# Attention followed by SwiGLU on one core: buffers laid out from both ends of SBUF, and a new order of the handover

## The chip, the cores and the metric

The kernel runs on one core of one Trainium2 chip. The metric is the device time of one execution in microseconds (us). Engines are named as the profile names them: PE is the matrix engine (PEld its weight loads), DVE the vector engine, ACT the scalar engine, POOL the GpSimd engine, SP the engine whose queue issues the DMAs (SPq). The five run side by side and wait for one another through semaphores only.

## The reference

Attention with rotary embedding over 4 batches of 8 heads (576 tokens, head size 64), and on its output, laid out as 2304 tokens of width 512, a gated feed-forward of width 1536:

```python
q_rot, k_rot = rotate(q), rotate(k)
scores = D ** -0.5 * q_rot @ k_rot.swapaxes(-1, -2)
scores = scores - scores.max(-1, keepdims=True)
attn = np.exp(scores); attn = attn / (attn.sum(-1, keepdims=True) + 1e-09)
x = (attn @ v).transpose(0, 2, 1, 3).reshape(B * S, H * D)     # 2304 x 512
g = x @ w_gate                                                  # 512 x 1536, float64 weights
out = (g * sigmoid(g) * (x @ w_val)) @ w_out                    # 1536 x 512
```

q, k and v are float32; the kernel is handed the three weight matrices as 64-bit numbers.

## The kernel before

Every product is made of three matmuls (or of two, where a stacked operand holds both parts) on operands cut in a high part `h` and a low part `l`: hi x hi, hi x lo, lo x hi. The cut is a copy to a narrower format (ACT, or POOL for x), and a subtraction.

**Attention.** Two heads make a pair; there are 16 pairs of 9 blocks of 128 queries, n = 0 to 143, p = n // 9 and b = n % 9. For each block PE makes the scores (`scores`, L351), DVE their maximum (`peak`, L366, tile nmt), ACT the exponential (`exp`, L384), PE four transposes (`trans`, L427), ACT the high part and DVE the low part of them (L428, L429, tiles ET1 and ET2). The products with v (`pv`, L467) stand in a list of closures, ten to a PSUM bank, and are taken from it a few in each block; ACT copies the result (`pv_evac`, L472, tile Y), and SP stores it to DRAM (`store`, L486 to L492, tensor yd). A small transpose and store of the reciprocal row sums follows each batch (`rstore`, tensor rd). While a pair runs, POOL rotates q and k two pairs ahead (`rope`) and splits the next v (`vsplit`); PE, ACT and DVE cut the next q and k, which eight DMAs rearrange (`qk_stack`, QK<-N). The buffers N, QK, BD and QZ exist twice, one set for even pairs, one for odd.

**Work for the feed-forward that runs beside attention.** The order in which it is taken stands in PLAN. `cl` and `cvs`: the two converted weight matrices of the first f-tile (f = 0, 128 of the 1536 columns) are loaded and converted in pairs 0 to 3 (`wfirst`). One conversion (`bits`, L608 to L616) turns a 64-bit weight tile into two 32-bit ones with six DVE operations, one ACT copy and two POOL operations. `xs` and `xe`: the first half of the tokens (s = 0, three tiles of 384, four chunks of 128 rows each) is loaded from yd and, with the reciprocals R from rd, made ready by four POOL operations per chunk (`xload`, `xprep`, L594 to L600), between pair 4 and the beginning of pair 15.

**The handover.** At n = 144 attention's tail is placed (the last transposes, the last two rounds of `pv`, the last `rstore`), from there on ACT and DVE issue in the order of the text; POOL does so all through. Then attention's pools are closed, the feed-forward's are opened in the memory that they held, and `first_group` runs f-tiles 0 and 1, with PE in the order of the text. It loads and converts the weights of f = 1 and both `w_out` tiles (`wconv`, each with its nine operations in line), loads the whole second half of the tokens (s = 1) into the accumulator tiles (`stage`, L550, acc<-yd, 768 KB for each of six DMAs) and makes it ready in steps called `scale` and `cut` on POOL, DVE and ACT. `gv` is one tile of the first layer: twelve matmuls g, twelve matmuls v (L660), then on ACT the activation sg (L665), on DVE h = v x sg (L666), on ACT the high and on DVE the low part (L669, L670). g and v have two PSUM buffers each, so a g two tiles on waits for sg, and a v for h. `down` is a tile of the second layer (L684).

**Groups 1 to 5** repeat `gv` and `down` for two f-tiles each, from about 390 us to the end.

Of the kernel before, what the change touches and what calls it, by code (L numbers as in the profile page):

```python
# [34 lines left out]
    order=["qk", "scores", "trans", "pv", "exp", "evac", "rstore", "rope", "tails", "conv", "x", "vsplit"],  # L35
# [67 lines left out]
class Attn:  # L103
    def __init__(self, tc, ctx, q, k, v, tab, yd, rd):
# [3 lines left out]
        pool = lambda name, bufs, **kw: ctx.enter_context(tc.tile_pool(name=name, bufs=bufs, **kw))  # L108
        self.tab_src = tab
        self.x_p = pool("a_x", 2)  # L110
        self.rot_p = pool("a_rot", 2)
        self.t_p = pool("a_t", 1)
        one = pool("a_one", 1)
        self.tab = one.tile([128, 2, 9, D], FP32, name="tabs")
        self.VR = one.tile([128, 10, D], FP32, name="VR")
        self.N, self.QK, self.BD, self.VS, self.QZ = [], [], [], [], []

        def pairbufs(i):
# [4 lines left out]
        pairbufs(0)  # L123
        self.VS.append(one.tile([128, 10, 128], F32R, name="VS0"))
# [3 lines left out]
        one = pool("a_two", 1)  # L128
        pairbufs(1)
# [16 lines left out]
        self.sc_p = pool("a_sc", 2, space=PS)  # L146
        self.tr_p = pool("a_tr", PLAN["trb"], space=PS)
        self.pv_p = pool("a_pv", 4 - PLAN["trb"], space=PS)
# [329 lines left out]
    def store(self, p, half, Y):  # L478
        d = self.nc.sync.dma_start
# [25 lines left out]
class Moe:  # L505
    def __init__(self, tc, keep, yd, rd, wg, wv, wo, out):
# [4 lines left out]
        self.xh = {0: xs.tile([128, NCH, SG], F32R, name="xh0")}  # L511
        self.xl = {0: xs.tile([128, NCH, SG], F32R, name="xl0")}
        self.ld_p = pool("m_ld", 2)
        self.r_p = pool("m_r", 1)
        self.R = None
        self.staged = {}
        self.wpool = xs
        self.Wb = [self.wbuf(0), None]
        self.W, self.Hh, self.Hl = {}, {}, {}

    def wbuf(self, k):
        return [[self.wpool.tile([128, 512], F32R, name=f"w{i}{x}{k}") for x in "hl"] for i in range(2)]

    def open(self, ctx):
        tc = self.tc
        pool = lambda name, bufs, **kw: ctx.enter_context(tc.tile_pool(name=name, bufs=bufs, reuse_waits="tile", **kw))
        self.raw_p = pool("m_raw", 3)
        self.ax_p = pool("m_ax", 2)
        self.wpool = pool("m_w1", 1)
        self.Wb[1] = self.wbuf(1)  # L530
        self.s_p = pool("m_s", 2)
        accs = [pool("m_acc0", 1)]
        self.h_p = [pool("m_h0", 1)]
        xs = pool("m_x1", 1)
        self.xh[1] = xs.tile([128, NCH, SG], F32R, name="xh1")
        self.xl[1] = xs.tile([128, NCH, SG], F32R, name="xl1")
        self.h_p.append(pool("m_h1", 1))
        accs += [pool(f"m_acc{t}", 1) for t in (1, 2)]
        self.wo_p = pool("m_wo", 3)
        PS = bass.MemoryType.PSUM  # L540
        self.g_ps = pool("m_g", 2, space=PS)
        self.v_ps = pool("m_v", 2, space=PS)
        self.d_ps = pool("m_d", 4, space=PS)
        self.acc = [a.tile([128, 6, DM], FP32, name="acc") for a in accs]

    def stage(self, t):
        X = self.acc[t].rearrange("p t d -> p (t d)").rearrange("p (g q) -> p g q", q=384)
        o = SG + t * 384
        for h in range(2):
            self.nc.sync.dma_start(out=X[64 * h:64 * h + 64],  # L550
                                   in_=self.yd[h, :, :, o:o + 384].rearrange("g d q -> d g q"))
        self.staged[t] = X

    def xload(self, s, c, t):
        nc = self.nc
        o = s * SG + t * 384
        if s == 0:
            X = self.ld_p.tile([128, 2, 384], FP32, name="Xab")
            for h in range(2):
                P = slice(64 * h, 64 * h + 64)  # L560
                nc.sync.dma_start(out=X[P], in_=self.yd[h, 2 * c:2 * c + 2, :, o:o + 384].rearrange("a d q -> d a q"))
        else:
            X = self.staged[t][:, 2 * c:2 * c + 2]
        if self.R is None or self.R[0] != (s, t):
            R = self.r_p.tile([128, NCH * 384], FP32, name="R").rearrange("p (c n) -> p c n", c=NCH)
            b0, b1 = 2 * s, 2 * s + 1
            parts = {0: [(b0, 0, 384, 0)], 1: [(b0, 384, 128, 0), (b1, 0, 256, 128)],
                     2: [(b1, 256, 256, 0), (b0, -1, 64, 256), (b1, -1, 64, 320)]}[t]
            for b, col, n, to in parts:
                for h in range(2):  # L570
                    rb = self.rd[b]
                    off, st = (512 * h + col, 1024) if col >= 0 else (4096 + 64 * h, 128)
                    src = bass.AP(tensor=rb.tensor, offset=rb.offset + off, ap=[[0, 64], [st, NCH], [1, n]])
                    nc.sync.dma_start(out=R[64 * h:64 * h + 64, :, to:to + n], in_=src)
            self.R = ((s, t), R)
        return X[:, 0], X[:, 1], self.R[1][:, c]

    def xscale(self, ld, eng):
        Xa, Xb, R = ld
        eng.tensor_tensor(out=Xa, in0=Xa, in1=Xb, op=ALU.add)  # L580
        eng.tensor_tensor(out=Xa, in0=Xa, in1=R, op=ALU.mult)

    def xcut(self, s, c, t, ld, eng):
        hi = self.xh[s][:, c, t * 384:(t + 1) * 384]
        lo = self.xl[s][:, c, t * 384:(t + 1) * 384]
        self.nc.scalar.copy(hi, ld[0])
        eng.tensor_tensor(out=lo, in0=ld[0], in1=r32(hi), op=ALU.subtract)

    def xprep(self, s, c, t, ld, eng):
        nc = self.nc  # L590
        Xa, Xb, R = ld
        hi = self.xh[s][:, c, t * 384:(t + 1) * 384]
        lo = self.xl[s][:, c, t * 384:(t + 1) * 384]
        eng.tensor_tensor(out=Xa, in0=Xa, in1=Xb, op=ALU.add)  # L594
        eng.tensor_tensor(out=Xa, in0=Xa, in1=R, op=ALU.mult)
        if eng is nc.gpsimd:
            eng.tensor_scalar(out=hi, in0=Xa, scalar1=1.0, scalar2=1.0, op0=ALU.mult, op1=ALU.mult)
        else:
            eng.tensor_copy(hi, Xa)
# [27 lines left out]
    def wops(self, f, i):  # L627
        nc = self.nc
        raw = self.raw_p.tile([128, 512, 2], U32, name="raw")
        X = self.ax_p.tile([128, 512], U32, name="X")  # L630
        if i < 2:
            src = (self.wg, self.wv)[i].bitcast(U32)[:, f * 256:(f + 1) * 256]
            nc.sync.dma_start(out=raw.rearrange("p (c f) t -> p c (f t)", c=NCH),
                              in_=src.rearrange("(c p) f -> p c f", p=128))
            hi, lo = self.Wb[f % 2][i]
        else:
            nc.sync.dma_start(out=raw.rearrange("p f t -> p (f t)"),
                              in_=self.wo.bitcast(U32)[f * 128:(f + 1) * 128, :])
# [3 lines left out]
        return self.bits(raw, X, hi, lo, nc.gpsimd)  # L642
# [5 lines left out]
    def gv(self, f, s, t):  # L648
        nc = self.nc
# [3 lines left out]
        sl = slice(t * 384, (t + 1) * 384)  # L653
        ps = [self.g_ps.tile([128, 512], FP32, name="g")[:, 0:384], self.v_ps.tile([128, 512], FP32, name="v")[:, 0:384]]
        for i in range(2):
            Wh, Wl = self.W[f, i]
            n = 0
            for c in range(NCH):
                for l, x in ((Wh, self.xh[s]), (Wh, self.xl[s]), (Wl, self.xh[s])):
                    nc.tensor.matmul(ps[i], l[:, c * 128:(c + 1) * 128], x[:, c, sl],  # L660
                                     start=(n == 0), stop=(n == 3 * NCH - 1))
                    n += 1
# [7 lines left out]
        nc.vector.tensor_tensor(out=lo, in0=h, in1=r32(hi), op=ALU.subtract)  # L670

# [31 lines left out]
def attn_swiglu(ctx: ExitStack, tc: tile.TileContext, q, k, v, wg, wv, wo, tab, out):  # L703
# [6 lines left out]
    if True:  # L710
        moe = Moe(tc, ctx, yd, rd, wg, wv, wo, out)
        with ExitStack() as actx:
            at = Attn(tc, actx, q, k, v, tab, yd, rd)
# [11 lines left out]
            xq = [(c, t) for t in range(3) for c in range(4)]  # L725
# [65 lines left out]
            def x(n, p, b):  # L791
                if [p, b] in P["xs"]:
                    c, t = xq.pop(0)
                    need = {c, ("r", 0)} | ({4 + c, ("r", 1)} if t else set())
                    assert need <= at.done
                    pend.append((c, t, moe.xload(0, c, t)))
# [47 lines left out]
def first_group(moe):  # L844
# [16 lines left out]
    def run(ops):  # L861
        for op in ops:
            op()
# [74 lines left out]
```

## Time and profile before

| what | value |
|---|---|
| median of 3 runs | 768.74 us (767.19 to 769.77) |
| profiled execution, device time | 767.48 us |
| its span in the trace | 765.7 us |
| mean granted PE clock over the span | 0.993 |
| PE busy | 730.3 us (95%) |
| DVE, POOL, ACT busy | 536.1, 350.6, 346.2 us |
| last pair of attention | about 274.0 to 290.7 us |
| handover, `first_group` | about 290.7 to 390 us |

The span is 1.8 us shorter than the device time of the same execution, which is 1.3 us below the median. In the rows further down, a time in brackets at the end of a row is how long the engine sat idle before the instruction, and behind the arrow stands what ended that idle time.

### The profile page before, as it was taken

The numbers are of one execution on the slowest core, as the hardware profiler recorded it, in microseconds if no ns is written. First come the engines' busy times: TensorE is split into PE (matmuls) and PEld (weight loads), VectorE is DVE, ScalarE is ACT, GpSimd is POOL, SyncE is SP. The second block draws the span as 40 slices with busy tenths as digits, with TensorE's granted clock in tenths as the row PEclk, the third lists the DMA queues.
The fourth block names the chain that finished last, engine by engine and source line by source line (L and its number), as shares of the span: only waits on it lengthen the run. The fifth ranks groups of instructions, "written<-read, shape, count | busy, mean of one in ns | idle before, by whom it ended". The sixth has DMA issues, their size and how long they took to land.

```text
span 765.7 us, 12531 instructions
## 1 busy us (share of the span) xinstructions
PE 730.3 (95%) x4506; PEld 689.1 (90%) x4506; DVE 536.1 (70%) x858; ACT 346.2 (45%) x809; POOL 350.6 (46%) x367
## 2 busy tenths in 40 slices
PE   7799999999999988679999999999999999999998
PEld 6698989999999988678899989998999899989996
DVE  6899878888888866677695675567566647653234
ACT  2788878888989874234333201320132022202210
POOL 5789868989989545662533311330142014201000
PEclk9999999999999999989999999999999999999999
DMA  7777788878877784950221010111011002000015
GB/s 198 190 207 205 189 204 212 213 207 230 214 194 180 191 240 110 216 139 1 82 83 56 28 56 27 56 49 36 27 56 58 26 28 73 10 1 1 1 68 179
DMA packets 79758, 86.95 MB, mean 114 GB/s; under 512 B 22848, under 2 KB 66768, under 8 KB 79696
## 3 DMA queue, kind: packets, MB, share of 16 engines
q1 hardware_dynamic: 79696, 86.15, 42.3%
q8 instruction: 36, 0.59, 0.3%
q14 instruction: 26, 0.21, 0.1%
HBM read 47.78 MB, written 14.23 MB: 81 GB/s over the span
## 4 chain that ended last, share of the span: by engine, by line
PE 79%; DMA 7%; DVE 6%; ACT 4%; SPq 2%; issue 1%; POOL 0%; DVEq 0%; POOLq 0%; ACTq 0%
PE d L684 19%; PE g L660 19%; PE v L660 18%; PE pv L467 8%; PE sc L351 7%; PE tr L427 6%; DMA raw<-in_moe_w_out_dram 2%; DMA QK<-N 2%; DMA yd<-Y 2%; ACT E L384 2%; DVE nmt L366 1%; PE tr L291 1%; DVE ET1l L429 1%; ACT N L310 1%; DVE ET2l L429 1%
## 5 line engine op out<-in xcount | busy, mean ns | idle before, releaser
L366 DVE TENSOR_REDUCE nmt<-sc 128x1 f32<-128x576 f32 x144 | 108.1, 752 | 25.5 <-PE sc L351 24.8
L669 ACT CAST Hh<-h 128x384 fp32r<-128x384 f32 x72 | 37.0, 515 | 172.7 <-DVE h L666 127.3
L660 PE MATMUL g<-xh,w0h 128*128 128x384 f32 x288 | 97.8, 340 | 14.6 <-ACT sg L665 14.6
L384 ACT ACTIVATE E<-sc,nmt 128x576 f32<-128x576 f32 x128 | 97.3, 760 | 8.2 <-DVE nmt L366 8.1
L660 PE MATMUL g<-xh,w0l 128*128 128x384 f32 x288 | 97.1, 337 | 0.0
L660 PE MATMUL g<-xl,w0h 128*128 128x384 f32 x288 | 97.1, 337 | 0.0
L660 PE MATMUL v<-xh,w1l 128*128 128x384 f32 x288 | 96.7, 336 | 0.2 <-POOL w1l L616 0.2
L666 DVE TENSOR_TENSOR h<-v,sg 128x384 f32<-128x384 f32 x72 | 40.0, 555 | 81.3 <-PE v L660 78.6
L660 PE MATMUL v<-xh,w1h 128*128 128x384 f32 x288 | 96.7, 336 | 0.0
L660 PE MATMUL v<-xl,w1h 128*128 128x384 f32 x288 | 96.5, 335 | 0.0
L689 DVE TENSOR_TENSOR acc<-d,acc 128x512 f32<-128x512 f32 (+1 forms) x91 | 61.6, 680 | 45.2 <-PE d L684 45.2
L684 PE MATMUL d<-Oh,Hl 128*128 128x512 f32 (+1 forms) x218 | 84.9, 389 | 0.0
L684 PE MATMUL d<-Ol,Hh 128*128 128x512 f32 (+1 forms) x218 | 84.9, 389 | 0.0
L684 PE MATMUL d<-Oh,Hh 128*128 128x512 f32 (+1 forms) x218 | 84.7, 389 | 0.0
L427 PE MATMUL tr<-ident,E 128*128 128x128 f32 x512 | 77.7, 276 | 0.5 <-DVE ET1l L429 0.4
L615 POOL TENSOR_TENSOR raw<-raw,w0h 128x512 f32<-128x512 f32 x11 | 14.7, 1333 | 137.1 <-ACT w0h L614 123.6
L615 POOL TENSOR_TENSOR raw<-raw,Oh 128x512 f32<-128x512 f32 x12 | 17.0, 1419 | 125.9 <-DVE Hl L670 76.0
L670 DVE TENSOR_TENSOR Hl<-h,Hh 128x384 fp32r<-128x384 f32 x72 | 50.3, 699 | 31.8 <-ACT Hh L669 31.8
L665 ACT ACTIVATE sg<-g 128x384 f32<-128x384 f32 x72 | 35.2, 489 | 79.9 <-PE g L660 79.4
L660 PEld LDWEIGHTS g<-xh,w0h 128*128 128x128 f32 x288 | 54.6, 190 | 16.6 <-ACT sg L665 16.2
L351 PE MATMUL sc<-QK 128*128 128x288 f32 x248 | 61.4, 329 | 6.6 <-DMA QK<-N 4.2
L427 PEld LDWEIGHTS tr<-ident,E 128*128 128x128 f32 x512 | 62.3, 142 | 2.6 <-PE tr L291 1.3
(130 smaller groups left out, 1847.0 us busy)
## 6 DMA issues: line engine op xcount, KB each, us to landing
QK<-N SPq DMA_DIRECT2D x64, 288.0 KB, 4.6
yd<-Y SPq DMA_DIRECT2D x32, 256.0 KB, 3.4
raw<-in_moe_w_out_dram SPq DMA_DIRECT2D x12, 512.0 KB, 3.2
raw<-in_moe_w_gate_dram SPq DMA_DIRECT2D x11, 512.0 KB, 3.5
raw<-in_moe_w_val_dram SPq DMA_DIRECT2D x11, 512.0 KB, 3.5
Xab<-yd SPq DMA_DIRECT2D x24, 192.0 KB, 3.6
acc<-yd SPq DMA_DIRECT2D x6, 768.0 KB, 8.4
X<-in_k_dram SPq DMA_DIRECT2D x16, 256.0 KB, 4.6
```

Source lines behind the costliest of these rows:

```text
L351: nc.tensor.matmul(ps[:, g, 0:288], l, rr[:, o + g * 288:o + (g + 1) * 288], start=(x == 0), stop=(x == len(terms) - 1))
L366: nc.vector.tensor_reduce(out=nmcol, in_=ps[:, :, 0:288], axis=AX.XY, op=ALU.max, negate=True)
L384: nc.scalar.activation(out=E.rearrange("p (a b) -> p a b", a=2), in_=ps[:, :, 0:288], func=ACTF.Exp, bias=nmcol, scale=1.0, accum_out=self ...
L427: nc.tensor.transpose(ps[:, c], E[:, o + c * 128:o + (c + 1) * 128], self.ident)
L467: nc.tensor.matmul(st["ps"][:, 0:w], VS[:, sl, :], t, start=(x == 0), stop=(x == last))
L660: nc.tensor.matmul(ps[i], l[:, c * 128:(c + 1) * 128], x[:, c, sl], start=(n == 0), stop=(n == 3 * NCH - 1))
L665: nc.scalar.activation(out=sg, in_=ps[0], func=ACTF.Silu)
L666: nc.vector.tensor_tensor(out=h, in0=ps[1], in1=sg, op=ALU.mult)
L669: nc.scalar.copy(hi, h)
L670: nc.vector.tensor_tensor(out=lo, in0=h, in1=r32(hi), op=ALU.subtract)
L684: nc.tensor.matmul(ps, l[:, tok], r[:, z], start=(n == 0), stop=(n == 3 * FG - 1))
L689: nc.vector.tensor_tensor(out=acc[:, z], in0=ps, in1=acc[:, z], op=ALU.add)
```

## The change

**Memory.** The buffers of even pairs, the tables, VR and the staging tiles of q and k (`a_pair0`, `a_x`, `a_rot`, `a_t`) are allocated from the right end of SBUF, all else of attention from the left. The right ones are closed at the start of pair 15, the last pair, which uses the odd set; in their place `open_early` puts the second weight buffer (Wb[1]), one staging tile of weights (raw0), a tile for the tokens s = 1, t = 0, the s and h tiles. The four PSUM banks of the scores are closed after the last block and given to g and v (`open_gv`), before the rest of attention has ended. The rest (`open_late`: raw1, w_out tiles, tokens s = 1, t = 1 and 2, the accumulators, d) is opened behind attention, each tile waiting for the tiles it replaces and not for whole pools. Raw tiles are two instead of three, each with its X inside.

**Work moved into the last pairs.** POOL makes 16 chunks of tokens instead of 12: nine in pairs 5 to 13, one each, three in pair 14 and the four new ones (s = 1, t = 0) in pair 15. The conversion of both weight tiles of f = 1 (`conv1`, list `c1`) goes into pair 15: its first load at b = 0, the second at b = 5, eleven of its twelve DVE operations within the pair.

**Handover.** From the end of n = 143 on, PE, ACT, DVE and SP all follow the text. PE goes: last transposes, tails, g of the first tile, ten pv, v of the first tile, ten pv, the transpose of the reciprocals, then the next tiles. The last store of Y and the last of rd are issued by ACT instead of SP. `first_group` makes the second half's tiles t = 1 and 2 in eight `xprep` with DVE (ACT for the copy), each chunk loaded by itself into one of two 384 KB buffers; `stage`, `xscale` and `xcut` are gone. The order of tiles is (f, s, t) = 000, 001, 002, 100, 101, 102, 010, 110, then `down` 0 to 8, then 011, 012, 111, 112, then `down` 9 to 17.

```diff
-    cl=[0, 12],
-    cvs=[2, 2, 3, 3, 4, 4, 5, 6, 8, 16, 17, 18, 19, 20, 21, 22, 24, 26],
-    xs=[[4, 6], [6, 6], [7, 7], [8, 4], [9, 5], [10, 4], [11, 5], [12, 5], [13, 4], [14, 1], [14, 2], [14, 8]],
-    xe=[[6, 2], [6, 7], [7, 7], [9, 0], [10, 3], [10, 7], [12, 1], [13, 7], [14, 2], [14, 4], [14, 7], [15, 1]],
+    cl=[0, 9],
+    cvs=[2, 2, 3, 3, 4, 4, 5, 6, 8, 12, 14, 16, 18, 20, 22, 24, 26, 28],
+    xs=[[4, 6], [5, 5], [6, 5], [7, 5], [8, 7], [9, 5], [10, 5], [11, 5], [12, 7], [13, 7], [14, 1], [14, 2],
+        [14, 8], [15, 0], [15, 2], [15, 4]],
+    xe=[[5, 3], [6, 3], [7, 3], [8, 3], [9, 3], [10, 3], [11, 3], [12, 3], [13, 5], [14, 1], [14, 3], [14, 5],
+        [15, 1], [15, 3], [15, 5], [15, 7]],
+    c1=[[0, 1, 1, 2, 2, 3, 3, 4, 4], [6, 7, 7, 8, 8]],
...
-        nc.sync.dma_start(out=self.rd[b], in_=rr)
+        (nc.scalar if b == B - 1 else nc.sync).dma_start(out=self.rd[b], in_=rr)
...
-        d = self.nc.sync.dma_start
+        d = (self.nc.scalar if (p, half) == (B * H // 2 - 1, 1) else self.nc.sync).dma_start
...
+            def conv1(n, p, b):
+                for i, at_ in enumerate(P["c1"]):
+                    if p == NP - 1 and b == at_[0] - (i > 0):
+                        cv1[i] = moe.wops(1, i, 0)
+                    for _ in range(at_.count(b) if p == NP - 1 else 0):
+                        tc.keep_in_program_order(cv1[i].pop(0)())
...
+                if (p, b) == (NP - 1, 0):
+                    early.close()
+                    moe.open_early(mctx)
...
+            ctl2 = tc.manual_schedule(engines={getattr(mybir.EngineType, e) for e in ("PE", "Activation", "DVE", "SP")})
+            ctl2.__enter__()
+            scx.close()
+            moe.open_gv(mctx)
+            at.trans(NB - 1)
+            at.pv_some(10)
+            at.pv_evac()
+            at.tails(NP - 1, 1)
+            ps = [moe.mm(0, 0, 0, 0)]
+            for op in cv1[1][:1 - len(cv1[1])]:
+                op()
+            at.pv_some(10)
+            at.pv_evac()
+            ps.append(moe.mm(0, 0, 0, 1))
+            at.pv_some(10)
+            at.pv_evac()
+            at.rstore(B - 1)
+            for op in cv1[1][1 - len(cv1[1]):]:
+                op()
+        moe.open_late(mctx)
+        first_group(moe, ps)
...
+    conv(0, 2, 1)
+    load(0, 1)
+    load(1, 1)
+    moe.ev(0, 0, 0, ps)
+    ps = mm(0, 0, 1)
+    conv(1, 2, 0)
+    cut(0, 2)
+    moe.rload(1, 1)
+    moe.ev(0, 0, 1, ps)
+    ps = mm(0, 0, 2)
+    cut(1, 2)
+    prep(0, 1)
+    load(2, 1)
+    moe.rload(1, 2, moe.acc[2][:, 0:3].rearrange("p t d -> p (t d)"))
+    moe.ev(0, 0, 2, ps)
+    ps = mm(1, 0, 0)
...
```

`conv` issues the load and the six DVE operations of a conversion, `cut` its ACT and POOL operations, `mm` the 24 matmuls of a tile, `ev` its four operations on ACT and DVE.

## Rows read from the trace of the kernel before

**Rows 1.** The page, part 1: busy us, share of the span, instructions.
```profile
PE 730.3 (95%) x4506; PEld 689.1 (90%) x4506; DVE 536.1 (70%) x858; ACT 346.2 (45%) x809; POOL 350.6 (46%) x367
```

**Rows 2.** Matmuls in order of time; PE's idle times over 1 us from 270 us on.
```profile
281.44 0.41 PE L467 MATMUL pv<-ET2h,VS 128*128 128x320 f32 x1 [2.58 <-ACT Y L472]
...
305.55 0.44 PE L660 MATMUL g<-xh,w0h 128*128 128x384 f32 x1 [2.88 <-ACT sg L665]
...
312.06 0.44 PE L660 MATMUL g<-xh,w0h 128*128 128x384 f32 x1 [2.07 <-ACT sg L665]
...
319.37 0.44 PE L660 MATMUL g<-xh,w0h 128*128 128x384 f32 x1 [2.37 <-ACT sg L665]
...
329.57 0.69 PE L660 MATMUL g<-xh,w0h 128*128 128x384 f32 x1 [5.75 <-ACT sg L665]
...
371.50 0.44 PE L660 MATMUL g<-xh,w0h 128*128 128x384 f32 x1 [1.54 <-ACT sg L665]
```

**Rows 3.** Busy us by stretch: PE, PEld, DVE, ACT, POOL, clock, DMA share, GB/s.
```profile
59.00:76.00 17.00, 16.34 (x124) 15.08 (x123) 16.01 (x26) 14.63 (x37) 16.37 (x19) 1.00 0.78 201
...
274.00:290.70 16.70, 14.12 (x112) 13.50 (x110) 11.68 (x20) 12.38 (x31) 3.57 (x4) 1.00 0.87 241
...
302.50:329.60 27.10, 13.85 (x75) 12.40 (x73) 17.43 (x26) 9.12 (x17) 15.63 (x13) 0.97 0.94 210
329.60:335.00 5.40, 5.40 (x17) 5.40 (x18) 4.78 (x6) 0.90 (x2) 5.24 (x5) 0.51 0.35 126
```

**Rows 4.** The chain that ended last: start us, us, what.
```profile
273.20 7.66 DMA yd<-Y
...
308.90 17.37 DMA raw<-in_moe_w_out_dram
...
329.57 4.21 PE g L660 x12
333.78 2.67 PE v L660 x12
336.45 2.08 PE g L660 x12
```

**Rows 5.** DMAs: issues on SP's queue in order of time; page 6, KB, us to landing.
```profile
272.33 0.35 SPq L637 DMA_DIRECT2D raw<-in_moe_w_out_dram x1
...
303.16 0.37 SPq L491 DMA_DIRECT2D yd<-Y  x1
...
raw<-in_moe_w_out_dram SPq DMA_DIRECT2D x12, 512.0 KB, 3.2
```

**Rows 6.** In order of time: conversion beside POOL (first and last of six), ACT, conversion alone.
```profile
296.58 0.62 DVE L608 TENSOR_SCALAR X<-raw 128x512 uint32<-128x512 uint32 x1
...
302.12 1.39 DVE L613 SCALAR_TENSOR_TENSOR X<-raw,X 128x512 f32<-128x512 uint32 x1
...
303.71 1.28 ACT L665 ACT_TABLE_LOAD   x1
305.01 0.49 ACT L665 ACTIVATE sg<-g 128x384 f32<-128x384 f32 x1
...
326.36 0.43 DVE L608 TENSOR_SCALAR X<-raw 128x512 uint32<-128x512 uint32 x1 [5.32 <-DMA raw<-in_moe_w_out_dram]
...
329.55 0.56 DVE L666 TENSOR_TENSOR h<-v,sg 128x384 f32<-128x384 f32 x1
```

**Rows 7.** In order of time: conversion operations during pair 0, a POOL operation beside one.
```profile
29.44 0.41 DVE L609 TENSOR_SCALAR R<-R 128x512 f32<-128x512 f32 x1
...
34.71 1.31 POOL L615 TENSOR_TENSOR R<-R,w0h 128x512 f32<-128x512 f32 x1 [3.28 <-ACT w0h L614]
...
35.10 1.47 DVE L613 SCALAR_TENSOR_TENSOR R<-R 128x512 f32<-128x512 uint32 x1
```

**Rows 8.** One chunk of tokens on POOL in order of time, first and last of four.
```profile
274.44 1.01 POOL L594 TENSOR_TENSOR Xab<-Xab 128x384 f32<-128x384 f32 x1 [0.96 <-DMA Xab<-yd]
...
277.24 1.01 POOL L600 TENSOR_TENSOR xl<-Xab,xh 128x384 fp32r<-128x384 f32 x1
```

More of the change, by code (lines that the diff above doesn't have):

```diff
@@ L34 @@
     warm=[10, 4, 2, 8],
-    order=["qk", "scores", "trans", "pv", "exp", "evac", "rstore", "rope", "tails", "conv", "x", "vsplit"],
+    order=["qk", "scores", "trans", "pv", "exp", "evac", "rstore", "rope", "tails", "conv", "x", "conv1", "vsplit"],
     qk0=[0, 2, 2],
@@ L519, in __init__ @@
+        self.Wb = [self.wbuf(xs, 0), None]
         self.W, self.Hh, self.Hl = {}, {}, {}
[L521 to L530, printed above, removed]
-        self.s_p = pool("m_s", 2)
[L532 to L538, printed above, removed]
-        self.wo_p = pool("m_wo", 3)
[L540 to L544, printed above, removed]
@@ new lines, in open_gv, with open_late, pool @@
+    def open_gv(self, ctx):
+        for a in "gv":
+            self.ps[a] = ctx.enter_context(self.tc.tile_pool(name=f"m_{a}", bufs=2, reuse_waits="tile",
+                                                             space=bass.MemoryType.PSUM))
+    def open_late(self, ctx):
+        def pool(name, bufs, **kw):
+            return ctx.enter_context(self.tc.tile_pool(name=name, bufs=bufs, reuse_waits="tile", **kw))
+        self.raw_p.append(pool("m_raw1", 1))
+        self.wo_p = pool("m_wo", 3)
+        self.h_p[1] = pool("m_h1", 1)
+        one = pool("m_x1", 1)
+        for t in (1, 2):
+            self.xbuf(one, t)
+        one = pool("m_acc", 1)
+        self.acc = [one.tile([128, 6, DM], FP32, name=f"acc{t}") for t in range(3)]
+        self.d_ps = pool("m_d", 4, space=bass.MemoryType.PSUM, side="right")
@@ new lines, in rload @@
+    def rload(self, s, t, into=None):
+        R = self.r_p.tile([128, NCH * 384], FP32, name="R") if into is None else into
+        R = R.rearrange("p (c n) -> p c n", c=NCH)
+        b0, b1 = 2 * s, 2 * s + 1
+        parts = {0: [(b0, 0, 384, 0)], 1: [(b0, 384, 128, 0), (b1, 0, 256, 128)],
+                 2: [(b1, 256, 256, 0), (b0, -1, 64, 256), (b1, -1, 64, 320)]}[t]
+        for b, col, n, to in parts:
+            for h in range(2):
+                rb = self.rd[b]
+                off, st = (512 * h + col, 1024) if col >= 0 else (4096 + 64 * h, 128)
+                src = bass.AP(tensor=rb.tensor, offset=rb.offset + off, ap=[[0, 64], [st, NCH], [1, n]])
+                self.nc.sync.dma_start(out=R[64 * h:64 * h + 64, :, to:to + n], in_=src)
+        self.R[s, t] = R
@@ L549, in stage, with xload @@
+    def xload(self, s, c, t):
+        o = s * SG + t * 384
+        X = self.ld_p.tile([128, 2, 384], FP32, name="Xab")
         for h in range(2):
             self.nc.sync.dma_start(out=X[64 * h:64 * h + 64],
[L551 to L587, printed above, removed]
+                                   in_=self.yd[h, 2 * c:2 * c + 2, :, o:o + 384].rearrange("a d q -> d a q"))
@@ L652, in gv, with ev @@
             self.Hl[f] = self.h_p[f % 2].tile([128, NT], F32R, name="Hl")
[L653 to L662, printed above, removed]
+        ps = self.ps["gv"[i]].tile([128, 512], FP32, name="gv"[i])[:, 0:384]
+        xh, xl = self.x[s, t]
+        Wh, Wl = self.W[f, i]
+        n = 0
+        for c in range(NCH):
+            for l, x in ((Wh, xh), (Wh, xl), (Wl, xh)):
+                self.nc.tensor.matmul(ps, l[:, c * 128:(c + 1) * 128], x[:, c],
+                                      start=(n == 0), stop=(n == 3 * NCH - 1))
+                n += 1
+        return ps
+    def ev(self, f, s, t, ps):
+        nc = self.nc
         sg = self.s_p.tile([128, 384], FP32, name="sg")
@@ L724, in attn_swiglu @@
             at.load_qk(2, True)
[L725 removed]
+            xq = [(s, c, t) for s, t in ((0, 0), (0, 1), (0, 2), (1, 0)) for c in range(4)]
             pend = []
```

235 lines of the change are left out of this document (117 added, 118 removed).

## The prediction, made before the changed kernel had run

> **What bounds the kernel now.** I read the page's busy times first. PE is busy 730.3 of 765.7 us [rows 1]: PE sets the time, and only the 35 us in which it idles, and what it does at a low clock, can be won. The work on PE is the same before and after. So the second view is PE in order of time, with the idle time before each matmul [rows 2]. What PE loses at the start and in single waits of the early pairs the change doesn't touch. From 270 us to the end six waits are longer than 1 us: one of 2.58 in the last pair of attention, four of 2.88, 2.07, 2.37 and 5.75 in the handover, one of 1.54 behind it. All but the first end with sg on ACT.
>
> The third view, busy time by stretch, says the same from the other side [rows 3]: from 302.5 to 329.6 PE is busy 13.85 of 27.1 us, so 13.25 us are lost (the four waits and small gaps). Behind the longest wait the granted clock is 0.51 of full speed, the lower level, 1.2 GHz. The chain of waits gives the price: twelve matmuls g take 4.21 us there and the v behind them 2.67, against 2.08 for twelve at full clock [rows 4]; (4.21 - 2.08) + (2.67 - 2.08) = 2.72.
>
> The same chain names the causes. The Y store issued at 273.20 took 7.66 us and held ACT's next copy, hence PE's 2.58; three weight loads of 512 KB had been issued just ahead of it [rows 4, 5]. The w_out load issued at 308.90 took 17.37 us, behind the 768 KB loads of all later tokens; DVE stood for it and with it h, sg and PE, 5.75 us. The three waits between come from conversions that stand in line ahead of sg and h: the first one's six DVE operations ran from 296.58 to 303.5, 6.9 us [rows 6].
>
> **What the change can take away.** 2.58 (last pair) + 13.25 (handover) + 2.72 (clock) + 1.54 (the wait at 371.5, whose tile now follows two conversions placed later, with only two tiles of `gv` behind it) = 20.1 us. The 768 KB loads are gone, the weights of f = 1 are ready before the handover, so what is left of the causes is w_out's two conversions.
>
> **What it adds, in the last pair.** PE is busy 14.12 us there, DVE 11.68 [rows 3]. Eleven of twelve conversion operations now come to DVE. Alone they are cheap: six of them, with the gaps, take 3.2 us (326.36 to 329.55) [rows 6], so eleven 5.8. Beside POOL they are not: the six at 296.58 took 6.9 us, so eleven 12.7. During pair 0, where POOL is busy about three quarters of the time, singles took from 0.41 to 1.47; the one of 1.47 began at 35.10 inside a POOL operation that ended at 36.02 [rows 7]. In the last pair POOL will have four chunks of 3.8 us [rows 8] and a conversion's two operations of 1.3: nearly 18 us, so it is almost always busy, but a DVE operation that begins between two POOL operations is not delayed. I take 0.65 us each, 7 us: nearer to pairs 0 to 2, where such operations stand singly among PSUM reads as they will here, than to the six in a row at 296.58. Then DVE has 11.7 + 7 = 18.7 us; where DVE bounds a pair it is busy some 94% (16.01 of 17.00 us in a pair with conversions) [rows 3], so the pair's work takes 19.8 against PE's 14.1: 5.7 us longer, and 4.5 if part of the eleven falls in the blocks in which DVE has spare time. I enter 5. Ends: 3 (5.8 us of operations, none delayed, (11.7 + 5.8) / 0.94 = 18.6, less what the spare blocks take) and 10 (12.7 us: (11.7 + 12.7) / 0.94 = 26, less the same).
>
> The Trainium skill bears on this (SBUF — State Buffer, section on two separate sides): VectorE and GpSimd share one pair of ports, an exclusive lock that whoever starts first holds for the whole instruction, while the other fully blocks. The operation at 35.10 agrees: 36.02 plus a bare operation is when it ended. By that rule alone, with POOL busy nine tenths of the pair and half an operation of POOL waited for each time, eleven operations would take about 10.5 us and I would enter 8 instead of 5, which gives 761 us as an estimate; that lies in the forecast's own range.
>
> **Late loads.** Both conversions use one staging tile, so the second load is issued only when POOL has ended the first, at about b = 5, with the first operation on it due at b = 6. A 512 KB load takes 3.2 us alone [rows 5], two blocks of 1.6 to 2 us. DVE takes its queue in order: an operation that waits for the load holds the maxima and low parts queued behind it, and PE with them. I enter 1 us for both loads; ends 0 and 5 (the 7.66 that the Y store needed in the same stretch when three loads went ahead of it, less 3.2).
>
> **What it adds, in the handover.** With T the end of the last pv: ACT has the Y copy (0.4), two stores and one of rd to issue (0.4 each by SP's issue of the same store [rows 5]; ACT issuing a DMA isn't in this trace, from 0.2 to 0.8 I would believe), the reciprocals (0.3), the w1 copy (0.7), the table load (1.28) and sg (0.49) [rows 6]: sg at T + 4.4. PE has one tile of 4.16 before it needs that: 0.3 lost. POOL's last conversion of f = 1 ends at T + 5.3, then the second w_out tile can be loaded into raw0, T + 8.7, and converted, T + 11.9. The h of tile 001 stands behind it on DVE, done at T + 12.4, and v of tile 100 needs its buffer at T + 10.9: 1.5 lost. The sg of tile 002 stands on ACT behind the copy of the first chunk, which waits for DVE: about 1.2 lost. From there DVE has 2 x 0.56 + 3 x 0.5 us a tile against 4.16 on PE. Sum 3. Ends: 1 (everything a little earlier) and 8 (the load lands 5 us later; each us goes straight to PE).
>
> **Moves entered at nothing.** The nine chunks in pairs 5 to 13: POOL did the same kind of work there, one chunk a pair at most times; if it fell late, `vsplit` behind it on POOL would hold pv, 0 to 1 us. The second conversion of f = 0 spread over pairs 1 to 3: the same operations among the same others. The stores of Y and rd no longer stand in SP's queue behind anything; SP's fixed order begins with the w_out load, whose memory (the odd N) is free when the last scores are done, some 8 us before T. Two raw tiles instead of three in groups 1 to 5: each has the time of two conversions to come free, more than 8 us, with PE two PSUM buffers ahead. Bounds for all of them -1 to +2; a gain is possible where a load no longer meets another.
>
> **Sum.** 20.1 - 5 - 1 - 3 = 11.1 us. Against the profiled execution: its 765.7 us span becomes 754.6, and its 767.48 us, which lie 1.8 above the span and 1.3 under the median, 756.4. On the median: 768.74 - 11.1 = 757.6.
>
> **The rivals.**
> - **DVE keeps up** (0.2). The eleven operations find DVE's gaps: the pair costs 2 instead of 5 and 1, the handover 2. Against it DVE's 11.68 busy us in a pair that PE needs 14.12 for; for it the singles of 0.41. 768.74 - 20.1 + 4 = 752.6.
> - **A new wait takes half** (0.2). DVE stands for the second load of the pair (5) and the second w_out tile (6), with the pair at 5: 768.74 - 20.1 + 16 = 764.6. For it: the staging tile's tight turn and DVE's order by text; against it: the 768 KB loads, gone from the queues, their bytes spread over some 50 us. That the freed memory is not free in time (tiles waiting for pools and not for tiles), so that the change wouldn't do what it says, comes out the same: the first w_out load would wait for attention's last store and cost 4 to 5 us.
> - **Slower** (0.07). One mechanism: DVE's queue in the last pair is stopped by a weight load that shares the DMA engines with chunks and the reciprocals, as w_out's 17.37 us [rows 4]. Such a load lands 14 us late, all of PE's attention waits: 768.74 - 20.1 + 5 + 14 + 3 = 770.6. It decides from about 12 us of lateness on. Against it: the pair's loads sum to some 2.5 MB (two weight tiles, three chunks of 384 KB, the reciprocals), spread by waits, and 2.5 MB move within 11 us at the 241 GB/s of that stretch [rows 3].
>
> **How the numbers follow.** The forecast's case has 0.53 and its own range is 754 to 761. With the rivals, eight times in ten the time lies between 752 and 766: the fast rival is just in, the half-gain one in, the slow one out. A measurement of this kernel tells about 0.3% (2.3 us) from no change, so faster means under 766.4. The forecast and the fast rival are under it wholly, the half-gain one for 0.16 of its 0.2, which leaves 0.04 for no change, with 0.02 of the slow one: 0.89 faster, 0.06 the same, 0.05 slower.
>
> **What would show it.** Right: no wait above 2 us on PE from 275 us on, clock 1.00 throughout, the last pair 18 to 20 us long with DVE busy over 90% of it, conversion operations of 0.4 to 1.4 there, two waits of 1 to 2 us ending with h or sg within 15 us of the last pv, and the 371-us wait gone. Wrong: PE idle in the last pair with DVE idle too (a load was late), PE waits in pairs 5 to 13 that were not there (POOL or SP order), or a clock below 1.00 behind a wait.

## The result, and the profile after

The changed kernel takes 759.24 us (median of 4 runs, 757.07 to 760.87) against 767.97 us (766.77 to 769.77) for the kernel before, run beside it: a ratio of 0.9883, 95% interval 0.9849 to 0.9916, or 8.7 us less. The profiled execution took 757.07 us, the lowest of the four, with a span of 755.3 us.

First the page's part 1 (busy us, share of the span, instructions), which answers [rows 1]: PE's busy time has hardly changed, and what it idles fell from 35.4 to 23.8 us.

```profile
PE 731.5 (97%) x4506; PEld 689.3 (91%) x4506; DVE 511.6 (68%) x870; ACT 344.2 (46%) x805; POOL 336.8 (45%) x359
```

Then matmuls in order of time, with the idle time ahead of them: all waits over 0.5 us from 270 us on, in the place of [rows 2].

```profile
279.55 0.53 PE L359 MATMUL sc<-QK 128*128 128x288 f32 x2 [0.99 <-ACT E L392]
...
294.22 0.41 PE L475 MATMUL pv<-ET2l,VS 128*128 128x320 f32 x1 [1.20 <-DVE ET2l L437]
...
304.18 0.45 PE L655 MATMUL g<-xh,w0h 128*128 128x384 f32 x1 [0.54 <-ACT sg L664]
...
312.36 0.44 PE L655 MATMUL v<-xh,w1h 128*128 128x384 f32 x1 [1.65 <-DVE h L665]
...
316.48 0.44 PE L655 MATMUL g<-xh,w0h 128*128 128x384 f32 x1 [1.76 <-ACT sg L664]
```

The waits of 2.58, 2.88, 2.07, 2.37, 5.75 and 1.54 us are gone; five short ones stand there. By stretch (columns as in [rows 3]): the last pair of attention with the block ahead of it, from the scores of block 134 to the first g; the handover; and what follows, in which PE is busy throughout at full clock. "The pair" below is that first stretch. (The last pair's own first scores stand at 270.12 us before and 268.64 after; the 274.0 of the table ahead of the prediction is the scores of its third block.)

```profile
267.49:290.55 23.06, 20.50 (x152) 18.56 (x151) 19.44 (x32) 17.73 (x45) 14.66 (x16) 1.00 0.69 190
290.55:318.00 27.45, 22.30 (x129) 21.01 (x128) 17.51 (x29) 7.90 (x15) 10.86 (x9) 1.00 0.35 101
318.00:400.00 82.00, 82.00 (x436) 77.12 (x435) 56.14 (x98) 30.69 (x62) 18.16 (x13) 1.00 0.31 90
```

Landmarks on PE that both profiled executions have divide the difference of the spans. The prediction's terms stand beside it.

| Stretch | before, us | after, us | difference | predicted |
|---|---|---|---|---|
| start to the scores of block 134 | 268.80 | 267.49 | -1.3 | 0 |
| to the first g (the pair) | 21.90 | 23.06 | +1.2 | -2.58 + 5 + 1 = +3.4 |
| to the first d of the second group | 147.44 | 134.77 | -12.7 | -13.25 - 2.72 - 1.54 + 3 = -14.5 |
| to the first d of the last group | 299.06 | 301.07 | +2.0 | 0 |
| to the end | 28.5 | 28.9 | +0.4 | 0 |
| sum | 765.7 | 755.3 | -10.4 | -11.1 |

The first line is spread, not effect: the eleven kernels below that are the changed one up to that point reach it between 266.60 and 270.59 us. For the fourth and the fifth the prediction had no term.

### The profile page after: what moved, and what is told of

It is laid out like the page before. It is cut to its first block, busy times and chain, and to the rows that moved or that the text cites. A ratio compares the mean times of both kernels' runs of the same rounds, so it can differ in the third digit from the quotient of the medians.

```text
span 755.3 us, 12540 instructions
## 1 busy us (share of the span) xinstructions
PE 731.5 (97%) x4506; PEld 689.3 (91%) x4506; DVE 511.6 (68%) x870; ACT 344.2 (46%) x805; POOL 336.8 (45%) x359
## 4 chain that ended last, share of the span: by engine, by line
PE 79%; DVE 5%; DMA 5%; issue 3%; POOL 3%; ACT 2%; SPq 1%; DVEq 0%; POOLq 0%
PE d L686 20%; PE g L655 19%; PE v L655 19%; PE pv L475 7%; PE sc L359 7%; PE tr L435 5%; DMA QK<-N 3%; PE tr L299 1%; ACT E L392 1%; DVE nmt L374 1%; ACT N L318 1%; POOL t L226 1%; DVE ET1l L437 1%; DMA raw<-in_moe_w_gate_dram 1%; POOL rot L230 1%
```

## The experiments

Theory: the gain is the sum of named stalls in two places, the last pair (where DVE becomes the bound) and the handover (where w_out's conversions are what is left). Rivals: the loads or POOL's share of the ports set the new times, or DVE's total work does whatever its order.

**What one queue order was worth.** In the kernel before, the 768 KB loads of all later tokens are put behind the second w_out load.

```diff
...
-    moe.stage(1)
-    moe.stage(2)
     moe.wconv(0, 2)
     moe.gv(0, 0, 2)
     moe.wconv(1, 2)
+    moe.stage(1)
+    moe.stage(2)
```

The rest of the edit holds these loads to the order of the text.

> The kernel before with one change in the order of its DMA queue: the 768 KB loads of the second and third tile of later tokens are issued behind the second w_out tile instead of ahead of it. Theory (the longest wait of 5.75 us and the low clock behind it, 2.72 us, come from that load landing 17.4 us late): the load lands within 5 us, the wait falls to 2 us or less, the clock stays at 1.00, and the total is 5 to 7 us below the kernel before, 761 to 763 us. Rival (the conversions in line ahead of sg cost the same whatever the load does, or the token loads now come late instead): total within 2 us of the kernel before.

763.21 us (10 runs), ratio 0.9934 (0.9913 to 0.9956): 5.4 us less. Of PE's long wait in the handover this is left (matmuls in order of time):

```profile
333.14 0.45 PE L662 MATMUL v<-xh,w1h 128*128 128x384 f32 x1 [1.12 <-DVE h L668]
```

The other waits of [rows 2] stay, with 2.25, 2.87, 1.95, 2.41 and 1.53 us. So the reading of the 5.75 us was right, and more than half of the gain is to be had by the order of one queue. Of the low clock it was right in part: where the long wait stood the clock is now 1.00 (329.6 to 345 us), but behind the wait of 2.41 it is 0.73 (319.59 to 326 us).

**The f = 1 conversion outside the last pair.** Both tiles are converted in the handover, w_out after them.

```diff
-    c1=[[0, 1, 1, 2, 2, 3, 3, 4, 4], [6, 7, 7, 8, 8]],
+    c1=[],
...
```

> The kernel after, with the whole conversion of both f = 1 weight tiles taken out of the last pair and put into the handover: the first tile's load is issued at the end of the pair and its six DVE operations stand behind the last low part of attention, the second tile is converted ahead of h of the first tile, and both w_out conversions move one place back. Theory (the last pair is bound by DVE because of the eleven conversion operations): the pair, from the scores of block 134 to the first g, goes from 22.9 back to about 18.5 us, the 1.2 us wait of the last pv goes too, and the handover loses 3 to 5 us to loads and conversions that stand ahead of h: 757 to 760 us, level with the kernel after. Rival (the pair's length is set by something else, the loads or POOL): the pair stays within 1 us of 22.9 and the total is 762 to 764 us.

762.85 us, ratio 0.9927 (0.99 to 0.9953). The pair is 19.18 us long (267.72 to 286.90) against 23.06, so the conversion with its loads costs it 3.9 us here, as the theory says. The total is the rival's, because the handover gives back more than that (matmuls in order of time; 0.69 us is a matmul at the lower clock, 0.45 one at full clock):

```profile
299.30 0.45 PE L655 MATMUL g<-xh,w0h 128*128 128x384 f32 x1 [0.77 <-ACT sg L664]
...
307.64 0.45 PE L655 MATMUL v<-xh,w1h 128*128 128x384 f32 x1 [1.79 <-DVE h L665]
...
318.28 0.69 PE L655 MATMUL g<-xh,w0h 128*128 128x384 f32 x1 [7.01 <-ACT sg L664]
```

These three are 9.57 us against 3.95. Converting in the pair pays, though the intervals of the two ratios still touch.

**POOL's chunks outside the last pair.** The last four chunks are made behind it.

```diff
-        [14, 8], [15, 0], [15, 2], [15, 4]],
+        [14, 8], [15, 0]],
-        [15, 1], [15, 3], [15, 5], [15, 7]],
+        ],
...
```

> The kernel after, with the four token chunks that POOL makes in the last pair made by POOL right behind that pair instead; conversions on DVE stay in the pair. Theory (in the pair the conversion operations are slowed by POOL's operations, which hold what both need): with POOL nearly idle in the pair the twelve operations go from 8.6 us (0.41 to 1.40 each) to about 6 (0.41 to 0.69), the pair from 22.9 to 20 to 21 us, and the handover's conversions on DVE become slower beside POOL instead: total 757 to 760 us. Rival (the operations' sum doesn't matter, DVE's waits do): operations fall to 6 us and the pair stays within 0.7 us of 22.9.

776.66 us, ratio 1.0123 (1.0077 to 1.0168): neither theory had it. The pair itself answers the question: 22.12 us against 23.06 with the same late load, so POOL's chunks and their loads beside DVE cost 0.9 us of the 3.9. The nine conversion operations ahead of TK2l take 5.1 us there and 7.3 in the changed kernel. The loss comes behind the pair (in order of time, SP's queue, DVE, PE):

```profile
308.02 4.92 SPq L582 DMA_DIRECT2D Xab<-yd  x4
...
313.03 0.54 SPq L635 DMA_DIRECT2D raw<-in_moe_w_out_dram  x1
...
317.93 0.81 DVE L604 TENSOR_SCALAR raw<-raw 128x512 uint32<-128x512 uint32 x1 [22.62 <-DMA raw<-in_moe_w_out_dram]
...
322.94 0.69 PE L655 MATMUL v<-xh,w1h 128*128 128x384 f32 x1 [17.25 <-DVE h L665]
```

SP's next token loads wait for buffers that POOL now frees late (one of them 17.5 us for xl); the w_out load stands behind them in SP's order, DVE's queue behind the load, h behind DVE. DVE's queue stopped by a late weight load is the prediction's slower rival, in another place and at 17 us; but here the load is late because it is issued late, not because it shares the DMA engines.

**A third staging tile.** The second w_out tile goes to memory that is free, and needn't wait for POOL.

```diff
-        tmp = self.raw_p[k].tile([128, 1536], U32, name="raw")
+        tmp = self.raw_p[k].tile([128, 1536], U32, name="raw") if k < 2 else self.acc[1][:, 0:3].rearrange("p t d -> p (t d)").bitcast(U32)
...
-    conv(1, 2, 0)
+    conv(1, 2, 2)
```

> The kernel after, with the second w_out tile loaded into a part of an accumulator tile that is still unused instead of the staging tile that the last f = 1 conversion holds until 305 us; nothing else changes. Theory (the two waits of 1.65 and 1.76 us on h and sg at 312 and 316 us come from that load being issued so late): the load is issued 10 us earlier, DVE doesn't stand for it, both waits go below 0.5 us, and the total is 2.5 to 3.4 us under the kernel after, about 756 us. Rival (they come from DVE's amount of work between sg and h, or from the reciprocals of the second half): DVE doesn't wait for the load any more and PE loses the same 3.4 us a little later, total within 1 us of the kernel after.

758.4 us, ratio 0.988 (0.9845 to 0.9915): no difference that can be told. DVE begins at 306.15 instead of 308.57, but now beside POOL (in order of time):

```profile
306.28 1.44 POOL L611 TENSOR_TENSOR raw<-raw,Oh 128x512 f32<-128x512 f32 x1 [0.87 <-DVE Hl L669]
306.61 1.40 DVE L605 TENSOR_SCALAR acc<-acc 128x512 f32<-128x512 f32 x1
307.80 1.39 POOL L612 TENSOR_TENSOR Ol<-raw 128x512 fp32r<-128x512 f32 x1
308.05 1.43 DVE L606 TENSOR_SCALAR acc<-acc 128x512 uint32<-128x512 uint32 x1
```

Each of the two takes 1.4 us, against 0.43 alone, and ends 0.3 us after POOL's. Of 2.4 us won, h comes 0.4 earlier, and PE's wait for it is 0.89 instead of 1.65. The Trainium skill (SBUF — State Buffer, section on two separate sides) says this of the ports that the two engines share: who comes second is blocked until the first has ended. These rows agree with it.

**The order at the end of attention.** w1's copy and sg go ahead of the last Y copy on ACT.

```diff
-            ps.append(moe.mm(0, 0, 0, 1))
+            ps += [moe.mm(0, 0, 0, 1), moe.s_p.tile([128, 384], FP32, name="sg")]
+            _ = [op() for op in cv1[1][-3:]]
+            nc.scalar.activation(out=ps[2], in_=ps[0], func=ACTF.Silu)
             at.pv_some(10)
             at.pv_evac()
             at.rstore(B - 1)
-            for op in cv1[1][1 - len(cv1[1]):]:
-                op()
...
```

> The changed kernel with ACT's order at the end of attention turned round: the copy of the last w1 tile of f = 1 (and with it POOL's two operations) and sg of the first tile stand ahead of the last Y copy, its stores and rd. In the changed kernel ACT idles 3.1 us ahead of that Y copy, and only after the stores makes the copy (301.68), so that POOL ends at 305.1 and the second w_out load is issued there. Theory (the waits of 0.54 for sg and 1.65 for h come from this order, by way of POOL and the staging tile): w1's copy at about 296.5, POOL ends at about 300, the w_out load is issued some 4.5 us earlier, both waits go, and the chunk behind it on DVE comes earlier too, so the 1.76 shrinks: 2.2 to 3.9 us faster than the changed kernel's 759.2, that is 755.3 to 757.0. Rival (the second w_out conversion is held by DVE and the ports shared with POOL, not by the load): at most 0.5 us, 758.7 or more, with h still waiting 1 us or more.

756.85 us, ratio 0.9855 (0.9827 to 0.9883). In the handover one wait is left, 1.42 us for sg; those of 0.54 and 1.65 are gone. They came from ACT's order by way of POOL and the staging tile. This is the lowest median of all, and in the theory's range, but its interval overlaps that of the changed kernel.

**The first chunk behind tile 002.**

```diff
-    prep(0, 1)
-    load(2, 1)
-    moe.rload(1, 2, moe.acc[2][:, 0:3].rearrange("p t d -> p (t d)"))
     moe.ev(0, 0, 2, ps)
+    prep(0, 1)
+    load(2, 1)
+    moe.rload(1, 2, moe.acc[2][:, 0:3].rearrange("p t d -> p (t d)"))
```

> The changed kernel with the first chunk of later tokens (two operations on DVE, a copy on ACT, one on DVE) placed behind sg and h of tile 002 instead of ahead of them; its tokens are needed only some 40 us later. Theory (PE's wait of 1.76 is sg standing on ACT behind the chunk's copy, which waits for DVE): the wait goes, those of 0.54 and 1.65 stay: 757.5. Rival (DVE is late whatever the order, and the tile behind it waits instead): the 1.76 reappears at the next tile, 759.2.

761.22 us, ratio 0.9917 (0.9893 to 0.9941). The rival's mechanism, at 2 us more than its time: the 1.76 us are back a tile later, at the lower clock (matmul in order of time), and the pair of its profile is 25.55 us long.

```profile
322.50 0.66 PE L655 MATMUL g<-xh,w0h 128*128 128x384 f32 x1 [1.86 <-ACT sg L664]
```

**Half of the second tile behind the pair.**

```diff
-    c1=[[0, 1, 1, 2, 2, 3, 3, 4, 4], [6, 7, 7, 8, 8]],
+    c1=[[0, 1, 1, 2, 2, 3, 3, 4, 4], [6]],
...
```

> The changed kernel with four of the six DVE operations of the second f = 1 tile moved out of the last pair, behind TK2l, where DVE later stands idle for 4.6 us; only the first operation stays. Theory (the last pair is bound by DVE, and each of its operations there goes into the time): the last wait of the pair, 1.20 for ET2l, goes, and PE starts the handover 1 to 2 us earlier, while w1's copy on ACT comes no later, being held by the stores: 1.2 to 2.2 us faster than 759.2, that is 757.0 to 758.0. Rival (DVE's sum up to w_out's conversion decides, not its order): the time comes back as a longer wait for sg or h in the handover, 759.2.

758.08 us, ratio 0.9881 (0.9858 to 0.9904), not to be told from the changed kernel. By the trace the 1.20 is gone, h waits 2.06 instead of 1.65, sg 0.20 instead of 1.76.

**All three edits.**

> The three edits together: ACT's turned order, the first chunk behind tile 002, four operations behind TK2l. Theory (the four waits left, 1.20, 0.54, 1.65 and 1.76, have three separate causes): nearly all 5.15 us go: 754 to 756. Rival (DVE's total work between the last scores and tile 100 is what is left, and any order only moves the wait): no more than 2 us, 757.2 or more.

757.3 us, ratio 0.9866 (0.9841 to 0.9891): the rival. Waits of 1.98 and 1.10 us for sg stand at two later tiles.

**The late first load.** The profiles so far showed one wait in the last pair that changed from kernel to kernel though nothing ahead of it had been edited. SP's queue, DVE and PE in order of time, in the changed kernel:

```profile
263.14 2.62 SPq L575 DMA_DIRECT2D R<-rd  x2
265.80 2.28 SPq L582 DMA_DIRECT2D Xab<-yd  x3
268.18 0.55 SPq L499 DMA_DIRECT2D yd<-Y  x1
268.77 0.47 SPq L500 DMA_DIRECT2D yd<-Y  x1
269.34 0.49 SPq L631 DMA_DIRECT2D raw<-in_moe_w_gate_dram  x1
...
275.98 0.84 DVE L604 TENSOR_SCALAR raw<-raw 128x512 uint32<-128x512 uint32 x1 [1.49 <-issue]
```

and in the kernel with ACT's turned order:

```profile
268.20 2.60 SPq L575 DMA_DIRECT2D R<-rd  x2
...
274.37 0.48 SPq L631 DMA_DIRECT2D raw<-in_moe_w_gate_dram  x1
...
281.07 0.55 DVE L604 TENSOR_SCALAR raw<-raw 128x512 uint32<-128x512 uint32 x1 [4.54 <-issue]
...
284.35 0.70 PE L359 MATMUL sc<-QK 128*128 128x288 f32 x2 [2.52 <-ACT E L392]
```

In both the load of the first f = 1 tile lands 6.5 us after its issue, and its issue is the last of a row that SP issues with hardly a gap from 252 us on, while the DMA engines are busy 0.93 of the time at 229 GB/s (252 to 270 us of the changed kernel); which of the two holds the other was not told apart. It comes late by 1.5 to 4.5 us, DVE stands for it, and the maxima behind it hold E and PE. (The rows give "issue" as the end of DVE's idle time, that is, no cause; that it is the load shows by DVE's start within 0.2 us of its landing, and by the run below.) The pair's length follows: 23.06 us with 1.49 of standing, 23.71 with 2.27 (third tile), 26.43 with 4.30 (stores on SP, below), 26.70 with 4.54. Hence a run with DVE's operations on this tile two blocks later, and four of the second tile's behind the pair as above:

```diff
-    c1=[[0, 1, 1, 2, 2, 3, 3, 4, 4], [6, 7, 7, 8, 8]],
+    c1=[[2, 2, 3, 3, 3, 4, 4, 4, 4], [6]],
...
-                    if p == NP - 1 and b == at_[0] - (i > 0):
+                    if p == NP - 1 and b == 5 * i:
...
```

> As the run with four operations behind TK2l (758.1), and the DVE operations of the first f = 1 tile begin two blocks later; its load is issued where it was. Six profiles show that load landing 6.5 us after its issue, while DVE, which takes its queue in order, stood 1.5 to 4.5 us for it ahead of the next maxima, and PE 1.0 to 2.6 us for E. Theory (the last pair's varying wait is this late load in DVE's queue): DVE's first operation finds its data, PE's waits of 1 to 2.6 us for E near the start of the pair go, and the sixth operation still ends in time: 755.5 to 757.5. Rival (what holds DVE is the sum of its work in the pair, so the operations moved later hold ET2l at the pair's end instead, or w_val, now issued behind w_out, comes late for h): 758 or more.

757.6 us, ratio 0.986 (0.9835 to 0.9885), not to be told from the changed kernel. The pair is 20.46 us long (it begins at 270.59, 3.1 us later), DVE doesn't stand for this load, and from 267 to 300 us PE is busy 32.27 of 33 us (29.24 in the changed kernel), by stretch:

```profile
267.00:300.00 33.00, 32.27 (x236) 30.91 (x235) 28.95 (x45) 22.16 (x58) 20.00 (x20) 1.00 0.66 184
300.00:330.00 30.00, 25.33 (x133) 23.92 (x132) 22.86 (x34) 9.82 (x20) 8.83 (x6) 0.94 0.50 133
```

So the mechanism is as said. But DVE stands 1.78 us for the second tile's load, which now lands behind the pair; that tile's operations then run beside POOL, most at 0.9 to 1.1 us each, and the handover's waits grow from 3.95 to 4.68 us, with a clock of 0.94. The same with ACT's turned order:

> The run before this one together with ACT's turned order (w1's copy and sg ahead of the last Y copy and its stores), without the chunk moved behind tile 002. Theory (late first load, DVE's operations in the pair and ACT's order at the end are separate causes): 759.2 less 2.4 less 1.2 less about 1 to 2: 753.5 to 755.5, with no wait above 1.5 us behind the pair. Rival (gains overlap on DVE, which has the same work to do between the last scores and tile 100): 756 or more.

758.73 us, ratio 0.9871 (0.9844 to 0.9897): the rival. From the scores of block 134 to the first d of the second group the changed kernel's profile takes 157.83 us, and those with ACT's turned order, half of the tile late, all three edits, the late first load and this one 157.28, 157.00, 157.24, 156.20 and 157.98. In them the pair is 2.6 us shorter to 3.6 us longer, and what follows makes up for most of it. That fits the rival's reading: DVE has a fixed amount of work there beside POOL, and an edit moves the wait. No run here changes that amount alone, so it is the likely cause and not a shown one.

**Two parts undone.** The last stores back on SP:

```diff
-        (nc.scalar if b == B - 1 else nc.sync).dma_start(out=self.rd[b], in_=rr)
+        nc.sync.dma_start(out=self.rd[b], in_=rr)
...
-        d = (self.nc.scalar if (p, half) == (B * H // 2 - 1, 1) else self.nc.sync).dma_start
+        d = self.nc.sync.dma_start
```

> The changed kernel with the last stores of Y and rd issued by SP again instead of ACT. In SP's fixed order they stand ahead of the first w_out load, which then waits for the last pv: issued at about 301 us instead of 287.4, landed at 304.6, converted on DVE by 308, and h of the first tile stands behind that on DVE. Theory (it is the queue that the store sits in that counts, not the half us that issuing it costs an engine): PE's first wait in the handover grows from 0.5 to 4 or 5 us: 763 to 765. Rival (DVE idles 4.6 us there, which covers the later load, and ACT is 1.4 us quicker): 758 to 760.

764.5 us, ratio 0.9933 (0.9904 to 0.9962). SP, DVE and PE in order of time:

```profile
303.69 0.36 SPq L499 DMA_DIRECT2D yd<-Y  x1
...
305.17 0.37 SPq L635 DMA_DIRECT2D raw<-in_moe_w_out_dram  x1
...
309.21 0.43 DVE L604 TENSOR_SCALAR raw<-raw 128x512 uint32<-128x512 uint32 x1 [8.94 <-DMA raw<-in_moe_w_out_dram]
...
313.00 0.59 PE L655 MATMUL v<-xh,w1h 128*128 128x384 f32 x1 [3.42 <-DVE h L665]
```

The w_out load goes out 18 us later than in the changed kernel (287.40), since it stands behind a store whose data isn't there yet. The Trainium skill (DMA: Bandwidth & Descriptors, section on issuing engines not being separate queues) says that issuing from several engines saves only the time of the issue. Here issuing the three costs ACT 1.4 us, and with them on SP the median is 5.3 us higher. In the handover PE waits 5.94 instead of 3.95 us at a clock of 0.94, and from the first g to the first d of the second group the profile takes 137.27 us instead of 134.77, 2.5 us more. The rest stands in a pair of 26.43 us, long by its late first load, ahead of which nothing was edited; how much of the median that is, no run tells. A queue is also an order.

PE and SP out of the fixed order:

```diff
-... ("PE", "Activation", "DVE", "SP")}
+... ("Activation", "DVE")}
```

> The changed kernel with PE and SP not in the fixed order from attention's tail on (ACT and DVE still are). The planner then issues the loads of the reciprocals ahead of the second w_out load, and starts g and v of the first tile ahead of the last pv. Theory (the fixed order of SP is what keeps w_out's second load ahead of some 20 smaller ones): that load comes 2 to 5 us later and h with it: 761.5 to 765. Rival (the order is worth nothing, as the prediction entered it): 758 to 760.

762.72 us, ratio 0.9932 (0.9909 to 0.9955). The size is the theory's (138.12 us from the first g to the first d of the second group, 3.4 more than in the changed kernel), the main cause isn't (in order of time):

```profile
304.86 0.42 ACT L480 COPY Y<-pv 128x320 f32<-128x320 f32 x1 [3.48 <-PE pv L475]
...
309.71 0.69 PE L655 MATMUL g<-xh,w0h 128*128 128x384 f32 x1 [4.89 <-ACT sg L664]
...
316.92 0.43 DVE L604 TENSOR_SCALAR raw<-raw 128x512 uint32<-128x512 uint32 x1 [5.21 <-DMA raw<-in_moe_w_out_dram]
```

The second w_out load is late, as expected, but costs PE at most the next wait, 1.08 us. The 4.89 come from PE's order: it takes v and the second tile ahead of attention's last pv, the last Y copy is 5.5 us later (304.86 against 299.39), and ACT makes sg behind it.

## Why the prediction was right, point by point

The forecast, 757.6 us, is 1.6 us under the measured median; on the pair of medians the gain was 8.7 of the 11.1 us forecast. The causes were right. That the number came so close is in part luck: in the profile the pair is 2.2 us shorter than its terms say, the handover's gain 1.8 us smaller, PE itself 2.4 us slower in the groups behind, and the start 1.3 us quicker by spread.

- **What bounds the kernel, and what goes.** Right. Every wait of [rows 2] went, the clock is 1.00 from 30 us on, and the third line of the table comes out once the waits that are left are counted: 17.51 less the waits of 5.15 now there is 12.4, measured 12.7. The cause named for the 5.75 us was shown alone.
- **Five us of DVE's work in the last pair.** The size of the two terms together was about right, the split wrong: the work was entered too high, "late loads" too low. The profiled pair lost 3.7 us (1.16 + 2.58), not 6, and over the prediction's own stretch (274.03 to 290.70 before, 272.10 to 290.55 after: 18.45 us, in its 18 to 20) 4.4. Of the eleven operations only seven had begun by the first g; the wait of 1.20 behind it belongs to the others, since it goes when four of them are moved, and makes it 4.9. The conversion with its late load took 2.9 of the pair, POOL's chunks 0.9, so the rule by which 8 was to be entered overstated them; operations took 0.41 to 1.40 us, as forecast. DVE was busy 19.44 of 23.06 us, 84%, not over 90%.
- **Late loads.** The term failed by its mechanism. I looked at the second load, behind the staging tile (DVE stood 0.98 us for it), and not at the first, which is late because SP's queue is. I had counted the pair's own bytes; what makes it late are the loads and stores of the pair ahead of it, which are still going out. Five of the profiles of kernels with the same beginning have DVE standing 2.4 us or more for it, with pairs up to 3.6 us longer than that of the profiled execution.
- **Three us in the handover.** 0.3, 1.5 and 1.2 were forecast, for the right instructions and causes; 0.54, 1.65 and 1.76 were measured, 3.95 in place of 3.
- **Moves entered at nothing.** The mechanism was named ("no longer stand in SP's queue behind anything") and rightly entered at nothing, since the change comes with it: the handover's gain rests on it, and without the stores' move or the fixed order 2.5 or 3.4 us of it are lost in the traces (5.3 or 3.5 by the medians).
- **"The work on PE is the same."** The step that failed. The same matmuls are there, but they take longer. In order of time, the first d of the second and third groups, before and after:

```profile
438.14 0.39 PE L684 MATMUL d<-Oh,Hh 128*128 128x512 f32 x1
...
512.91 0.39 PE L684 MATMUL d<-Oh,Hh 128*128 128x512 f32 x1
```

```profile
425.32 0.39 PE L686 MATMUL d<-Oh,Hh 128*128 128x512 f32 x1
...
500.59 0.39 PE L686 MATMUL d<-Oh,Hh 128*128 128x512 f32 x1
```

One group of work, with PE never waiting, takes 74.77 us before and 75.27 after. Over the groups that is the table's +2.4 us, a cost that the prediction entered at nothing. It is also what the gain by the medians fell short by, but the other lines of the table differ from their terms by as much.

## What to carry to other kernels

Read the queue that issues DMAs like an engine: a load is late when what stands ahead of it is, and an engine that takes its instructions in order passes that on to work that has nothing to do with the load. Work moved into idle time is cheap as long as the engine has idle time there; where one engine has no idle time left, most reorderings here only moved the wait. And a change of the memory layout should be checked in a stretch where nothing waits: here the instructions themselves took longer there, for a reason that is still open.

## What the runs showed of the hardware that was not expected

PE's rate at full clock differs between the two kernels. By groups of instructions from 400 to 750 us, one line of each (busy us, mean ns of one, idle), before and after:

```profile
L684 PE MATMUL d<-Ol,Hh 128*128 128x512 f32 x163 | 63.8, 392 | 0.0
```

```profile
L686 PE MATMUL d<-Ol,Hh 128*128 128x512 f32 x178 | 70.3, 395 | 0.0
```

Matmuls of g and v have 334 to 335 ns before and 336 to 337 after. A group takes 74.77 us in the traces of the kernel before and of its variant and 75.27 in those of the changed kernel and of its eleven variants, each within 0.03 us. Of the eleven token tiles of a group that the changed kernel's PE takes in one run of 24 matmuls g and v, three take 4.23 to 4.25 us (492.11 to 496.35 for one), two 4.19, and six 4.16 to 4.17 (483.79 to 487.95 for one); in the kernel before all ten such tiles of a group take 4.16. The matmuls, their shapes and the granted clock are the same; what differs is where the operands lie and in which tiles, what the other engines do meanwhile, and the order in which PE takes g, v and d in the first third of a group. Two of these don't fit. Inside an unbroken run of 24 the order is the same in both kernels. And the longer tiles aren't those with more going on: the tile from 483.79 takes 4.16 us with DVE busy 4.13 us of it, the one from 462.88 takes 4.23 with DVE busy 2.46 us and no DMA traffic. That leaves the place of the operands as the likely cause. It was not tried, and neither was which property of the place it is.
